# Moving y and its states ahead of the next chunk's scores, with the states in a bank of the w_out parts

## The chip, the cores and the metric

The kernel runs on one core of one Trainium2 chip. The metric is the device time in microseconds of one execution. Engines are named as in the profile: PE is TensorE, DVE is VectorE, ACT is ScalarE, POOL is GpSimd, SP is SyncE.

## The reference

A gated linear recurrence is followed by a two-layer block. Cut to what matters:

```python
batch, n_heads, seq, head_dim = (4, 8, 768, 48)
for t in range(S):
    state = alpha[:, :, t, :, None] * state + np.einsum('bhd,bhe->bhde', k[:, :, t], v[:, :, t])
    y[:, :, t] = np.einsum('bhd,bhde->bhe', q[:, :, t], state)
x = np.ascontiguousarray(y.transpose(0, 2, 1, 3)).reshape(B * S, H * D)   # 3072 x 384
h = x @ w_in                                                              # 384 -> 2048
g = h * (1.0 / (1.0 + np.exp(-h)))
out = g @ w_out                                                           # 2048 -> 384
```

## The kernel before

The recurrence is cut into 24 chunks of 128 tokens (6 along the sequence, times 4 batch entries; chunk n belongs to batch n mod 4). For a chunk the kernel works in stages, each a function:

- `products(n)` and `quotient(n)` build decayed keys and queries on VectorE (transposes at L708, scans at L734 and L764, products at L749, L751 and L770);
- `flip(n)` and `land(n)` turn the keys through a VectorE transpose (L780) and two transfers by way of DRAM, into `kn`;
- `scores(n)` multiplies keys by queries on TensorE, in tiles of 48 rows by 64 columns (the profile shows `ps_a<-p,kp 48*64`). ScalarE copies the result to `g` (L818, L821), GpSimd masks it (L825), and ScalarE scales the state `st` (L836);
- `values(n)` makes y: `g` times v and the old state times the queries, in tiles 128*32 (`ps_a<-g,vn` and `ps_a<-p,st`). ScalarE copies y to `xt` (L863);
- `states(n)` multiplies v by `kn`, also in tiles 128*32 (`ps_a<-vn,kn`), into a PSUM bank, and two VectorE adds (L880) put it onto `st`. The last four chunks need no states.

The two layers work on groups of four chunks. They are cut into pieces of a size: a piece of `enter` (the w_in side; 12 matmuls of 128x256 into banks `ps_m`) and a piece of `leave` (the w_out side; 16 matmuls of 128x192 into the two banks `ps_o`). Both are fast matrix-multiplication schemes with fewer products and more sums; the sums run mostly on VectorE (L958, L1033, L1047, L582 to L587). One `leave` has seven pieces, and two halves of a group have one `leave` each. Its bank use is: parts 1, 3 in bank 0; 2 in bank 1; 4 and 6 in bank 1; 5 and 7 in bank 0.

PSUM has eight banks: three `ps_a` for the recurrence, three `ps_m`, two `ps_o`.

The order is written out by hand. The outer loop runs over steps of four slots. In a slot come first the recurrence's stages of that slot, then `fill(step, slot)`, which issues pieces from a list until a due amount of work is reached. From the ninth chunk on, the slots of a step hold:

```python
stages = [[(land, 1), (scores, 1)], [(products, 0)], [(quotient, 0)],
          [(values, 1), (states, 1), (flip, 0)]]
```

The second number is the lag: at step s, `scores` treats chunk s-1. `marks` gives the slots at which a phase of the list ends; in the later phases 28 pieces, `leave` and `enter` in turn, are spread over 16 slots. A piece also has a chunk count that must have been bridged (its y made) before it may run. VectorE also audits the inputs in the spare time (L697, issued by `audits`). From the ninth chunk on TensorE is held to the order of the program (`keep_in_program_order`); the instructions of the other engines are put in order by a scheduler that works from estimated times, except where they are held as well.

Of the kernel before, what the change touches and what calls it, by code (L numbers as in the profile page):

```python
# [355 lines left out]
def quotients(  # L356
# [38 lines left out]
    C = 128  # L395
# [6 lines left out]
    NT = B * NCH  # L402
    CH = C // 2
    W = C + 1
    GB = 4
# [26 lines left out]
    def out_bank(i, n):  # L432
        return outs[i].tile([128, 512], F32, name="ps_o")[:, 0:n]

    def ps_attn(n=C):
        return ps_a.tile([128, 512], F32, name="ps_a").rearrange("p (j c) -> p j c", c=n)
# [18 lines left out]
    NA = 2 * GB  # L455
# [133 lines left out]
    def sums_w(pair, upto):  # L589

        r = slice(2 * pair, 2 * pair + 2)
        while sums_done[pair] < min(upto, len(SUMS_W)):
            to, sa, a, sb, b = SUMS_W[sums_done[pair]]
            tc.keep_in_program_order(
                combine(block_w(to)[:, r], sa, block_w(a)[:, r], sb, block_w(b)[:, r]))
            sums_done[pair] += 1
# [246 lines left out]
    def values(n):  # L843
# [17 lines left out]
        if e == 0:  # L861
            xts[half] = xtp.tile([128, NKT, TB], F32, name="xt")
        act.copy(xts[half][:, :, e * C : (e + 1) * C], py[:, 0:NKT])  # L863
    def states(n):
        c = ctxs.pop(n)
        ci, b, vn = c["ci"], c["b"], c["v"]
        if ci < NCH - 1:

            ps = ps_attn()
            for j in range(NP):  # L870
                for i in range(4):
                    r = slice(32 * i, 32 * i + 32)
                    kn = c["kn"][:, j, r] if n < NA else c["kn"][:, i, 32 * j : 32 * j + 32]
                    pe.matmul(ps[r, j, 0:D], lhsT=kn, rhs=vn[:, 2 * j + i // 2, 0:D],
                              start=True, stop=True)
            for u in range(2):
                r = slice(64 * u, 64 * u + D)
                s, x = st[b][r, :, u, :], ps[r, :, 0:D]
                if ci > 0:
                    dve.tensor_tensor(s, x, s, ALU.add)  # L880
                else:
                    act.copy(s, x)
# [28 lines left out]
    def enter_plain(grp, h, pair):  # L911

        if h == 0:
            g_tiles(grp, pair)
        xt = xts[2 * grp + h]
        for f in range(8 * pair, 8 * pair + 8, 2):
            ps = bank(f // 2 % 3).rearrange("p (e n) -> p e n", e=2)
            for e in range(2):
                for t in range(NKT):
                    pe.matmul(ps[:, e, :], lhsT=w_in[:, t, (f + e) * 128 : (f + e + 1) * 128],  # L920
                              rhs=xt[:, t, :], start=(t == 0), stop=(t == NKT - 1))
            q, i = divmod(f, 4)
            act.activation(gts[grp, h, pair][:, i : i + 2, q % 2, :], ps, AF.Silu)  # L923
            if grp == 1 and pair == h == 0:
                differences(f // 2)
                differences(4 + f // 2)
            if grp > 0 and f % 8 == 6:
                side_by_side(grp, h, pair)
            yield
# [94 lines left out]
    def cells(grp, h, pair, m, k):  # L1024

        return gts[grp, h, pair][:, k::2, :, m * C : (m + 1) * C]
# [8 lines left out]
    def leave(grp, h):  # L1035


        def product(ps, m, k, w, first=False):
            for i in range(HF):
                q = i // 2  # L1040
                x = gts[grp, h, q // 2][:, 2 * (i % 2) + k, q % 2, m * C : (m + 1) * C]
                pe.matmul(ps, lhsT=x, rhs=w[:, i], start=(first and i == 0), stop=(i == HF - 1),
                          skip_group_check=True)

        def subtract(to, x, y):
            for pair in range(NQ // 2):
                dve.tensor_tensor(cells(grp, h, pair, *to), cells(grp, h, pair, *x),  # L1047
                                  cells(grp, h, pair, *y), ALU.subtract)

        def store(m, c, x, y=None):  # L1050
            ci, b = divmod(GB * grp + 2 * h + m, B)
            o = opool.tile([128, HO], F32, name="o")
            if y is None:
                act.copy(o, x)
            else:
                dve.tensor_tensor(o, x, y, ALU.add)  # L1056
            r = b * S + ci * C

            (gps if grp < NG - 1 else nc.sync).dma_start(out[r : r + C, c * HO : (c + 1) * HO], o)  # L1059

        u1, u2, u3, u4 = [rpool.tile([128, HO], F32, name=f"u{j}") for j in range(4)]
        steps = iter(range(7))

        def done():
            if 2 * grp + h in (1, 2):
                sums_w(2 * grp + h - 1, 4 * next(steps) + 4)

        def new(i):
            return out_bank(i, HO)

        a, b = new(0), new(1)
        product(a, 0, 0, b11, True)
        act.copy(u1, a)
        subtract((0, 0), (1, 0), (0, 0))
        done()
        yield
        product(b, 1, 0, t1, True)
        act.copy(u4, b)  # L1078
        done()
        yield  # L1080
        product(a, 0, 1, b21)
        store(0, 0, a)
        subtract((0, 1), (0, 1), (0, 0))
        done()
        yield
        b = new(1)
        product(b, 0, 0, t2, True)
        dve.tensor_tensor(u2, b, u1, ALU.add)
        subtract((1, 0), (1, 1), (0, 0))
        dve.tensor_tensor(u2, u2, u4, ALU.add)  # L1090
        done()
        yield
        a = new(0)
        product(a, 0, 1, b22, True)
        store(0, 1, a, u2)
        done()
        yield
        product(b, 1, 0, b12)
        dve.tensor_tensor(u3, b, u1, ALU.add)
        store(1, 1, u3, u4)  # L1100
        done()
        yield
        a = new(0)
        product(a, 1, 1, t4, True)
        store(1, 0, a, u3)
        done()
        yield
# [13 lines left out]
    def plain(grp, h, pair):  # L1121
        return (enter_plain(grp, h, pair), 12, 2 * (2 * grp + h) + 2)

    def group(grp):
        return [[(enter(grp, pair), 12, GB * grp + GB)] * 7 for pair in range(2)]

    def output(grp):
        return [[(leave(grp, h), 12, GB * grp + GB)] * 7 for h in range(2)]

    def both(x, y):  # L1130
        for i in range(max(len(x), len(y))):
            pieces.extend(x[i : i + 1] + y[i : i + 1])

    pieces = []
    for h in range(2):
        for pair in range(2):
            pieces += [plain(0, h, pair)] * 4
    pieces += [plain(1, 0, 0)] * 4 + [(leave(0, 0), 12, GB)] * 7
    phases = [len(pieces)]
    pieces += [plain(1, 1, 0)] * 4  # L1140
    both([(leave(0, 1), 12, GB)] * 7, [plain(1, 0, 1)] * 4 + [plain(1, 1, 1)] * 4)
    phases.append(len(pieces))
    before = output(1)
    for grp in range(2, NG):
        sums = sums_x(grp)
# [11 lines left out]

    def go_on():

        nonlocal done  # L1160
        next(pieces[done][0], None)
        done += 1

    audits = audit()
    done, bridged = 0, 0
    STEPS = NT + 1
    SLOTS = 4

    marks = [2 * SLOTS + 2] + [(GB * i + 2 * GB) * SLOTS + 3 for i in range(len(phases))]

    def settle():

# [29 lines left out]

    for step in range(STEPS):
        if step == 1:
            load(NIN)
        stages = [[(scores, 1)], [(products, 0)], [(values, 1)], [(states, 1)]]
        if step == 1:

            stages = stages[1::-1] + stages[2:]
        elif step >= NA:  # L1210
            stages = [[(land, 1), (scores, 1)], [(products, 0)], [(quotient, 0)],
                      [(values, 1), (states, 1), (flip, 0)]]
        for slot, group in enumerate(stages):
            for stage, lag in group:
                n = step - lag
                if not 0 <= n < NT:
                    continue
                stage(n)
                if stage is values:
                    bridged = n + 1  # L1220
                if stage is states and n + 1 + NIN < NA:
                    load(n + 1 + NIN)
                if stage is states and n + NV < NT:
                    load_v(n + NV)
            if step * SLOTS + slot == (NA + 1) * SLOTS - 1:
                x = decayed.rearrange("p (o i c) -> p o i c", o=2, c=C)
                for r, o in later:
                    gps.memset(x[r, o, :, 0:CH], 0.0)
            fill(step, slot)
            if step * SLOTS + slot >= NA * SLOTS - 1 and conv_done[1] == NFT and not late:  # L1230
                settle()
    while next(audits, 0) is None:
        go_on()
# [13 lines left out]
    for _ in range(5):  # L1247
        go_on()
    ps = ps_attn()[0:1, 0, 0:1]
# [64 lines left out]
```

## Time and profile before

| | us |
|---|---|
| median of 3 runs | 556.86 |
| lowest, highest | 556.4, 557.57 |
| profiled execution, its own time | 557.26 |
| span of that execution in the profile | 555.5 |

The page gives the busy time of each engine as a share of the span. A line of the timeline gives start and duration in microseconds, engine, line of the kernel, operation, output and inputs, for a matmul the tile (rows*columns of the array in use), shapes, and how many instructions were merged into the line; in brackets the idle time ahead of it and what ended it. A matmul's end is modelled, so the distance between two starts says more than a duration. A line of the waits gives who waited for whom, the sum in microseconds, how often, and the longest.

### The profile page before, as it was taken

The page shows a single profiled execution, that of the slowest core. Times are in us where ns is not written, and L with a number is a line of the kernel's source. Part 1 is how long each engine was busy: PE and PEld are TensorE (multiplying, and loading weights), DVE is VectorE, ACT ScalarE, POOL GpSimd, SP SyncE. Part 2 cuts the span into 40 slices and gives each one's busy share as a digit, 9 for nine tenths or more (in the row PEclk, how much of TensorE's full clock was granted, in tenths as well). Part 3 has the DMA queues.
Part 4 walks back from the last instruction along what each step waited for, and adds up shares of the span by engine and source line. Part 5 has one row for each costly group of instructions (what it writes and reads, how often), then busy time and mean ns, then how long its engine had stood idle before and what let it go on. Part 6 is the DMA issues. An engine that isn't in the chain of part 4 may idle for free. (4 is left out here: it accounts for less than half of the span.)

```text
span 555.5 us, 12640 instructions
## 1 busy us (share of the span) xinstructions
PE 541.4 (97%) x5026; PEld 489.7 (88%) x5026; DVE 445.4 (80%) x801; ACT 208.5 (38%) x466; POOL 76.1 (14%) x146
## 2 busy tenths in 40 slices
PE   6999999999999999999999999999999999999996
PEld 4788887998899999899999999988998999999996
DVE  5897788974999899997998986998884796945431
ACT  2556653223333253353353353344263342332100
POOL 3210000222210212021011021021121000001000
PEclk9999999999999999999999999999999999999999
DMA  9998971164454625355545654617642135500000
GB/s 215 246 249 210 232 195 33 47 161 116 117 136 125 159 63 138 86 145 149 139 112 139 193 139 120 191 27 183 170 137 91 54 91 169 172 11 22 10 24 30
DMA packets 99217, 70.09 MB, mean 126 GB/s; under 512 B 56272, under 2 KB 88656, under 8 KB 99152
## 3 DMA queue, kind: packets, MB, share of 16 engines
q1 hardware_dynamic: 97232, 65.30, 45.1%
q0 software_dynamic: 1920, 3.93, 2.0%
q8 instruction: 40, 0.66, 0.5%
q14 instruction: 25, 0.20, 0.1%
HBM read 61.34 MB, written 7.86 MB: 125 GB/s over the span
## 5 line engine op out<-in xcount | busy, mean ns | idle before, releaser
L388 PE MATMUL ps_o<-w_out,g 128*128 128x192 f32 x768 | 134.0, 328 | 0.5 <-DVE o L1056 0.5
L388 PEld LDWEIGHTS ps_o<-w_out,g 128*128 128x128 f32 x768 | 125.6, 190 | 3.5 <-DVE o L1056 1.0
L388 PE MATMUL ps_m<-xt,w_in 128*128 128x256 f32 x480 | 113.6, 383 | 1.5 <-ACT xt L863 1.1
L388 PEld LDWEIGHTS ps_m<-xt,w_in 128*128 128x128 f32 x480 | 89.1, 190 | 14.4 <-ACT xt L863 1.6
L388 PE MATMUL ps_o<-wt,g 128*128 128x192 f32 x576 | 99.7, 326 | 0.0
L388 PEld LDWEIGHTS ps_o<-wt,g 128*128 128x128 f32 x576 | 95.1, 190 | 1.6 <-issue 0.2
L388 PE MATMUL ps_m<-xc,w_in 128*128 128x256 f32 x288 | 70.7, 382 | 0.0
L388 PEld LDWEIGHTS ps_m<-xc,w_in 128*128 128x128 f32 x288 | 53.7, 190 | 7.0 <-DVE g L958 0.3
L1047 DVE TENSOR_TENSOR g<-g 128x512 f32<-128x512 f32 x72 | 50.1, 709 | 8.3 <-PE ps_o L388 8.3
L955 ACT ACTIVATE g<-g 128x1024 f32<-128x1024 f32 x32 | 33.1, 1056 | 61.2 <-DVE g L958 61.1
L1059 POOL DMA_DIRECT2D out_dram<-o x40 | 22.0, 551 | 219.5 <-DVE o L1056 113.7
L825 POOL TENSOR_SCALAR_AFFINE_SELECT g<-g 64x256 f32<-64x256 f32 x64 | 34.9, 546 | 124.4 <-ACT g L818 105.7
L388 PE MATMUL ps_m<-xc,wx 128*128 128x256 f32 x192 | 50.1, 383 | 1.0 <-DVE xc L586 1.0
L950 ACT COPY g<-ps_m 128x512 f32<-128x512 f32 x64 | 36.6, 588 | 37.0 <-PE ps_m L388 36.9
L388 PEld LDWEIGHTS ps_m<-xc,wx 128*128 128x128 f32 x192 | 35.2, 190 | 5.2 <-ACT u L1078 1.2
L958 DVE TENSOR_TENSOR g<-ps_m,g 128x512 f32<-128x512 f32 x56 | 37.1, 683 | 3.2 <-PE ps_m L388 2.7
L734 DVE TENSOR_TENSOR_SCAN u<-al,one 128x516 f32<-128x516 f32 x24 | 29.8, 1240 | 11.9 <-ACT al L731 11.6
L923 ACT ACTIVATE g<-ps_m 128x512 f32<-128x512 f32 x32 | 19.1, 597 | 41.7 <-PE ps_m L388 41.4
L950 ACT COPY part<-ps_m 128x512 f32<-128x512 f32 x32 | 18.9, 590 | 38.0 <-PE ps_m L388 24.0
L697 DVE TENSOR_REDUCE seen<-bits 128x1 f32<-128x512 int32 (+1 forms) x33 | 26.3, 823 | 5.7 <-DMA bits<-in_moe_w_in_dram 5.7
L764 DVE TENSOR_TENSOR_SCAN p<-al,inv 128x516 f32<-128x516 f32 x24 | 29.9, 1247 | 1.0 <-PE ps_a L388 0.3
L1056 DVE TENSOR_TENSOR o<-ps_o,u 128x192 f32<-128x192 f32 x24 | 8.5, 355 | 25.7 <-PE ps_o L388 22.8
(129 smaller groups left out, 648.5 us busy)
## 6 DMA issues: line engine op xcount, KB each, us to landing
bits<-in_moe_w_in_dram SPq DMA_DIRECT2D x24, 512.0 KB, 4.7
bits<-in_moe_w_out_dram SPq DMA_DIRECT2D x16, 384.0 KB, 3.9
at<-in_alpha_dram SPq DMA_DIRECT2D x64, 96.0 KB, 2.5
kt<-in_k_dram SPq DMA_DIRECT2D x64, 96.0 KB, 2.6
qt<-in_q_dram SPq DMA_DIRECT2D x64, 96.0 KB, 2.7
bits<-in_alpha_dram SPq DMA_DIRECT2D x9, 512.0 KB, 4.0
out_dram<-o POOLq DMA_DIRECT2D x40, 96.0 KB, 2.4
flips<-turn SPq DMA_DIRECT2D x12, 256.0 KB, 2.4
```

The lines of the kernel that those rows point to most:

```text
L388: in_order(nc.tensor.matmul(*args, **kw))
L697: dve.tensor_reduce(seen[kind][which][:, i : i + 1], x, axis=AX, op=op, apply_absolute_value=True))
L734: dve.tensor_tensor_scan(u[:, end - 1 :: -1], sg[:, end:0:-1], one[:, end:0:-1], 0.0, ALU.mult, ALU.add)
L764: dve.tensor_tensor_scan(p[:, 0:end], sg[:, 0:end], iv[:, 0:end], 0.0, ALU.mult, ALU.add)
L825: gps.affine_select(x, x, pattern=[[0, NP], [1, CH]], compare_op=ALU.is_ge, fill=0.0, base=0, channel_multiplier=-1)
L923: act.activation(gts[grp, h, pair][:, i : i + 2, q % 2, :], ps, AF.Silu)
L950: act.copy(to, ps)
L955: act.activation(x, x, AF.Silu)
L958: dve.tensor_tensor(to, a, b, op)
L1047: dve.tensor_tensor(cells(grp, h, pair, *to), cells(grp, h, pair, *x), cells(grp, h, pair, *y), ALU.subtract)
L1056: dve.tensor_tensor(o, x, y, ALU.add)
L1059: (gps if grp < NG - 1 else nc.sync).dma_start(out[r : r + C, c * HO : (c + 1) * HO], o)
```

## The change

From step 10 on, `values(n)` and `states(n)` have lag 2 and stand at the head of slot 0, immediately ahead of `land` and `scores` of the next chunk; before they stood in slot 3 of the step before, with one call of `fill` between. `states` then takes its bank from the w_out parts' two banks instead of from `ps_a`: bank 0 where three, four or five parts of the current `leave` have been issued, else bank 1. A counter `left` keeps how many that are. Where one or four parts have been issued and the next piece is again a part of w_out, that piece is issued first. There is one more step, and the marks from the second on move by one slot.

```diff
-    def states(n):
+    def states(n, behind=False):
...
-            ps = ps_attn()
+            if behind:
+                ps = out_bank(0 if left in (3, 4, 5) else 1, 512).rearrange("p (j c) -> p j c", c=C)
+            else:
+                ps = ps_attn()
...
+    leaves = []
+
+    def last(grp, h):
+        leaves.append(leave(grp, h))
+        return [(leaves[-1], 12, GB * grp + GB)] * 7
...
-        nonlocal done
+        nonlocal done, left
+        if pieces[done][0] in leaves:
+            left = left % 7 + 1
         next(pieces[done][0], None)
         done += 1
...
-    STEPS = NT + 1
+    STEPS = NT + 2
...
-    marks = [2 * SLOTS + 2] + [(GB * i + 2 * GB) * SLOTS + 3 for i in range(len(phases))]
+    marks = [2 * SLOTS + 2] + [(GB * i + 2 * GB) * SLOTS + 3 + (i > 0) for i in range(len(phases))]
...
         elif step >= NA:
-            stages = [[(land, 1), (scores, 1)], [(products, 0)], [(quotient, 0)],
-                      [(values, 1), (states, 1), (flip, 0)]]
+            lag = 2 if step > NA else 1
+            y = [(values, lag), (states, lag)]
+            stages = [[(land, 1), (scores, 1)], [(products, 0)], [(quotient, 0)], [(flip, 0)]]
+            stages[0 if lag == 2 else 3][0:0] = y
...
-                if not 0 <= n < NT:
+                if not 0 <= n < NT or lag == 2 and n < NA:
                     continue
-                stage(n)
+                if stage is values and lag == 2 and left in (1, 4) and pieces[done][0] in leaves:
+                    go_on()
+                if stage is states:
+                    states(n, lag == 2)
+                else:
+                    stage(n)
```

More of the change, by code (lines that the diff above doesn't have):

```diff
@@ L1125, in group @@
         return [[(enter(grp, pair), 12, GB * grp + GB)] * 7 for pair in range(2)]
+    leaves = []
+    def last(grp, h):
+        leaves.append(leave(grp, h))
+        return [(leaves[-1], 12, GB * grp + GB)] * 7
     def output(grp):
-        return [[(leave(grp, h), 12, GB * grp + GB)] * 7 for h in range(2)]
+        return [last(grp, h) for h in range(2)]
     def both(x, y):
@@ L1137, in quotients @@
             pieces += [plain(0, h, pair)] * 4
-    pieces += [plain(1, 0, 0)] * 4 + [(leave(0, 0), 12, GB)] * 7
+    pieces += [plain(1, 0, 0)] * 4 + last(0, 0)
     phases = [len(pieces)]
     pieces += [plain(1, 1, 0)] * 4
-    both([(leave(0, 1), 12, GB)] * 7, [plain(1, 0, 1)] * 4 + [plain(1, 1, 1)] * 4)
+    both(last(0, 1), [plain(1, 0, 1)] * 4 + [plain(1, 1, 1)] * 4)
     phases.append(len(pieces))
@@ L1164, in quotients @@
     audits = audit()
-    done, bridged = 0, 0
-    STEPS = NT + 1
+    done, bridged, left = 0, 0, 0
+    STEPS = NT + 2
     SLOTS = 4
-    marks = [2 * SLOTS + 2] + [(GB * i + 2 * GB) * SLOTS + 3 for i in range(len(phases))]
+    marks = [2 * SLOTS + 2] + [(GB * i + 2 * GB) * SLOTS + 3 + (i > 0) for i in range(len(phases))]
     def settle():
```

## The prediction

> **What bounds the kernel now.** I read the page first (busy shares), then the timeline of TensorE over one step, then its waits, then the timeline of VectorE behind the same step.
>
> ```profile
> PE 541.4 (97%) x5026; PEld 489.7 (88%) x5026; DVE 445.4 (80%) x801; ACT 208.5 (38%) x466; POOL 76.1 (14%) x146
> ```
>
> TensorE is full almost throughout, but its busy time is modelled, so I look at the distances between starts. One step in the middle:
>
> ```profile
> 327.90 2.76 PE L388 MATMUL ps_o<-w_out,g 128*128 128x192 f32 x16
> 330.50 1.89 PE L388 MATMUL ps_m<-xc,w_in 128*128 128x256 f32 x8
> 332.23 1.03 PE L388 MATMUL ps_m<-xt,w_in 128*128 128x256 f32 x4
> 333.09 2.76 PE L388 MATMUL ps_o<-wt,g 128*128 128x192 f32 x16
> 335.79 1.08 PE L388 MATMUL ps_a<-g,vn 128*32 128x128 f32 x32
> 336.68 0.84 PE L388 MATMUL ps_a<-p,st 128*32 128x128 f32 x24
> 337.34 0.52 PE L388 MATMUL ps_a<-vn,kn 128*32 128x48 f32 x32
> 337.80 1.13 PE L388 MATMUL ps_m<-xc,wx 128*128 128x256 f32 x4
> 338.76 1.89 PE L388 MATMUL ps_m<-xc,w_in 128*128 128x256 f32 x8
> 340.58 0.90 PE L388 MATMUL ps_a<-p,kp 48*64 48x128 f32 x32
> ```
>
> The first column is the start. Inside full-array work the pitch is steady: 8 matmuls of 256 columns in 330.50 to 332.23, 1.73 us or 0.216 each; 16 of 192 in 327.90 to 330.50, 2.60 us or 0.1625 each. The three groups 128*32 are y and states of chunk 18; the group 48*64 is the scores of chunk 19. Between them stands one piece of 12 matmuls, from 337.80 to 340.58: 2.78 us where 12 x 0.216 is 2.60. So 0.19 us is lost at its two borders, about half on entering (the first matmul's weights are not loaded ahead) and half on leaving. The same stretch in the steps where it is a piece of w_out (316.39 to 319.19) takes 2.80 for 2.60, 0.20 lost. TensorE waits for others very little after 140 us:
>
> ```profile
> PE ps_m L388 <- DVE xc L586: 1.0, 1, 1.0
> PE ps_a L388 <- DVE p L770: 0.5, 1, 0.5
> PE ps_m L388 <- DVE g L958: 0.4, 1, 0.4
> ```
>
> Measured as starts against pitch these are 1.2 us at 367, 0.55 at 143 and 0.93 around 229. So the bound is TensorE's own stream; what shortens it shortens the run, and what makes it wait lengthens the run.
>
> VectorE is the engine next to it, and runs behind:
>
> ```profile
> 336.56 1.16 DVE L708 STREAM_TRANSPOSE al<-at 128x512 f32<-128x512 f32 x1
> 337.75 1.23 DVE L734 TENSOR_TENSOR_SCAN u<-al,one 128x516 f32<-128x516 f32 x1
> ...
> 339.51 1.23 DVE L764 TENSOR_TENSOR_SCAN p<-al,inv 128x516 f32<-128x516 f32 x1
> 340.66 0.70 DVE L880 TENSOR_TENSOR st<-ps_a,st 48x192 f32<-48x192 f32 x2
> ```
>
> The two adds of L880 read the states' bank. TensorE finished it by 337.80; they end at 341.36, 3.56 us later. Today nothing waits for them soon.
>
> **What the Trainium skill says.** "TensorEngine Tiling (Array Packing)", Key Properties: changing the tiling mode drains TensorE. The trace agrees: 0.19 to 0.20 us at the borders of each full-array stretch. "TensorE: Matmul & The Clock Gate", Part 2: a weight load can be pulled ahead of running matmuls, matmuls keep their order. The trace agrees: no load cost shows inside a stretch, only at its start. "PSUM — Partial Sum Buffer", PSUM bank collisions: guard by bank and quadrant, not by address. So a w_out product must wait until VectorE has read the states out of its bank; no line of before shows that wait. "Perfetto Trace Analysis", Identifying the Most-Contended Engine: matmul busy share is a poor measure; hence the starts.
>
> **The change part by part.**
>
> *Removed.* Per chunk TensorE today leaves full-array work twice: for y+states and for scores. With y(n), states(n), scores(n+1) back to back, it leaves once. The full stretch between goes and its matmuls join a neighbour at pitch. The merged pairs are y(8) with scores(9) to y(22) with scores(23): 15. Gain 15 x 0.193 = 2.9 us. The drain from 128*32 to 48*64 stays: both groups keep their present lengths (2.01 and 0.83 us). No trace row has these two modes touching, so I bound it: a free switch would also save the tile side's drain, about 0.11 us (the first w_out start comes 0.15 after the last four states matmuls begin, these groups of four being 0.04 apart), 1.6 us in all; a switch dearer by 0.1 would cost 1.5 us. I take zero.
>
> *Moved.* y and states come one slot later; SP's transfers behind states (the three of v, for two chunks ahead) and the ScalarE copy of xt go with them. v is needed two steps later as before; the four kn transfers of `land` now stand right behind states, with a whole step before their reader. The POOL masks have 7 pieces, not 6, between scores and y. `quotient`, `products` and `flip` now come 2 pieces earlier in a step (one piece, not three, between scores and products), so scores(n+1) is later relative to its inputs. All lie beside TensorE's 20.5 us per step. The marks move by a slot with y, so each step still has 7 pieces. Cost nil; if VectorE were late this is where it would first show. An extra step at the end makes the last phase's first fills 4 instead of 1, from pieces that the loop after would issue anyway: nil.
>
> *Added: a wait.* States sit in a w_out bank, and the next product into it waits for L880; everything of TensorE queues behind that product, in order, and after it ScalarE and VectorE. Pieces alternate w_out, w_in. At 28 pieces per 16 slots, odd steps end with seven w_out parts done: bank 1 is free, and its next user is two w_out parts away: 0.83 (scores) + 2.60 + 0.11 + 2.60 = 6.1 us after states. The lags of L880 there are 4.0, 4.6, 2.3, 3.4 and 3.3 us (chunks 11 to 19): no wait. Even steps end with four done: bank 0 is free, but the fifth part wants it after scores and one w_in piece: 0.83 + 2.71 = 3.54 us. The lags of before, from the end of states to the end of L880, are 5.00 (chunk 12), 1.65 (14), 4.19 (16), 3.56 (18). Waits: 1.46 + 0 + 0.65 + 0.02 = 2.1 us. Chunk 8 has the same spacing, but there TensorE itself waits for p at 143 and L880 follows 0.8 us behind; nil. Chunks 20 to 23 have no states. Against that, a wait at chunk 12 lets VectorE catch up by 1.46 just ahead of the 0.93 us that TensorE lost to it around 229: that goes, minus 0.9. Net +1.2 us. Bounds: 0 if L880 lands earlier in VectorE's order, 5 if one more scan (1.23) gets ahead of it each time.
>
> *Sum* against the profiled execution's own 557.26 (span 555.5 and 1.8 around it): 557.26 - 2.9 + 1.2 = 555.6. That execution was 0.4 above the median of 556.86, so 555.2 against the median.
>
> **The rivals.**
>
> R1, *the bank gives all back*: the waits come to 2 to 4 us net; 556 to 558. For it: VectorE has 79.3 us of work in the 84 us from 190 to 274. Against: the waits of before, carried over, come to 2.1.
>
> R2, *slower, by the same bank*: in even steps one more 1.23 us scan is ordered ahead of L880. Lags 6.2, 2.9, 5.4, 4.8; waits 2.7 + 0 + 1.9 + 1.3 = 5.9, minus 0.9: 557.26 - 2.9 + 5.0 - 0.4 = 559.0. It decides at a mean lag of about 4.5 us in even steps; before has 3.6. For it: the transposes and scans of later chunks already run ahead of L880, and products now stand two pieces nearer. Against: at chunks 16 and 18 the whole chain al, u, p is already ahead.
>
> R3, *no waits at all* (VectorE's earlier quotient and flip leave it nearer to TensorE): 553.6 to 554.
>
> R4, *it does not do what it says*: if TensorE's order were the scheduler's, the groups need not touch. In this part of the kernel TensorE is kept in program order, so I give it no weight of its own.
>
> **How the numbers follow.** Forecast (554.2 to 555.7) 0.45, R3 0.11, R1 0.24, R2 and slower 0.20. A measurement can tell about 0.2%, 1.1 us. Faster by more: 0.56; within: 0.24; slower: 0.20. Range from 553.3 (R3) to 558.9 (R2's size).
>
> **What would show it.** Right: 128*32 groups followed at once by 48*64, 15 times; full stretches of 28 pieces' pitch with one 0.19 border per step; waits of TensorE's ps_o for `st` L880 of about a microsecond in even steps only. Wrong: such waits over 1.5 us each, or in odd steps; a longer 48*64 group (the switch costs); new waits for xc or g at L958 over those of before.

## The result, and the profile after

The change makes the kernel slower: 571.7 us median (571.32 to 572.26, 5 runs) against 556.4 us before (555.96 to 557.57, the three runs of the table above and two more); the ratio is 1.027, 95% interval 1.0259 to 1.0281. The profiled execution took 572.26 us with a span of 570.5, against 557.26 and 555.5 before: 15.0 us more of span.

From the page after, the busy shares, and the group of matmuls whose idle time has grown (busy time, mean ns of one, then the idle time before it and what ended most of it):

```profile
PE 543.5 (95%) x5026; PEld 493.3 (86%) x5026; DVE 445.3 (78%) x801; ACT 209.6 (37%) x466; POOL 74.2 (13%) x146
...
L388 PE MATMUL ps_m<-xc,wx 128*128 128x256 f32 x192 | 52.4, 397 | 10.2 <-DVE xc L586 10.2
```

The work is what it was; TensorE waited for the sums of x (`xc`), 10.2 us where it was 1.0. TensorE's own waits (total, times, longest) say the same and name the next one:

```profile
PE ps_m L388 <- DVE xc L586: 10.2, 2, 5.8
...
PE ps_a L388 <- DVE p L770: 2.9, 2, 1.9
```

TensorE's timeline from y of chunk 15 on, where group 3 starts:

```profile
274.26 1.08 PE L388 MATMUL ps_a<-g,vn 128*32 128x128 f32 x32
275.15 0.84 PE L388 MATMUL ps_a<-p,st 128*32 128x128 f32 x24
275.81 0.52 PE L388 MATMUL ps_o<-vn,kn 128*32 128x48 f32 x32
276.26 0.90 PE L388 MATMUL ps_a<-p,kp 48*64 48x128 f32 x32
277.10 2.87 PE L388 MATMUL ps_o<-w_out,g 128*128 128x192 f32 x16
279.80 1.89 PE L388 MATMUL ps_m<-xc,w_in 128*128 128x256 f32 x8
281.53 1.03 PE L388 MATMUL ps_m<-xc,wx 128*128 128x256 f32 x4
282.39 2.76 PE L388 MATMUL ps_o<-wt,g 128*128 128x192 f32 x16
290.93 1.62 PE L388 MATMUL ps_m<-xc,wx 128*128 128x256 f32 x3 [5.78 <-DVE xc L586]
```

Its first four lines are the change: y, states (now in `ps_o`) and scores stand together, and take 2.84 us in all, as long as they took apart. The last line is the loss: by the pitch of the 16 matmuls ahead of it that matmul was due at 284.99, and it started at 290.93.

The balance from the starts of TensorE's matmuls, each against the pitch of its kind (0.2165 us for 256 columns, 0.1625 for 192), before and after, in us:

| | before | after | difference |
|---|---|---|---|
| full-array stretches after 126 us (each costs 0.19 at its borders) | 33 | 18 | -2.9 |
| starts of groups 3 and 4: what the stretch with the wait for `xc` takes over the 18.37 of such a stretch undisturbed (before: over 15.77, in one of the two) | 1.2 | 8.2 + 6.3 | +13.3 |
| scores waiting for p (chunks 9, 10, 11) | 0.55 | 1.9 + 0.2 + 1.1 | +2.7 |
| smaller waits | | | +0.7 |
| last matmul's start | 550.45 | 564.22 | +13.8 |
| from there to the end of the span | 5.07 | 6.31 | +1.2 |

VectorE's timeline after, at the same place:

```profile
278.49 0.36 DVE L883 TENSOR_TENSOR st<-ps_o,st 48x192 f32<-48x192 f32 x1
...
283.89 0.69 DVE L1050 TENSOR_TENSOR g<-g 128x512 f32<-128x512 f32 x1
284.50 1.21 DVE L697 TENSOR_REDUCE seen<-bits 128x1 f32<-128x1024 f32 x1
285.63 0.42 DVE L582 TENSOR_TENSOR xc<-xt 128x256 f32<-128x256 f32 x1
...
290.38 0.41 DVE L586 TENSOR_TENSOR xc<-xc,xt 128x256 f32<-128x256 f32 x1
```

and before, where y of chunk 15 stood 1.8 us earlier:

```profile
276.76 0.42 DVE L582 TENSOR_TENSOR xc<-xt 128x256 f32<-128x256 f32 x1
...
281.80 0.42 DVE L586 TENSOR_TENSOR xc<-xc,xt 128x256 f32<-128x256 f32 x1
...
284.27 1.21 DVE L697 TENSOR_REDUCE seen<-bits 128x1 f32<-128x1024 f32 x1
```

L586 at 290.38 and 281.80 is the sixth sum, which TensorE's wait ends on. Before, the reduce of an audit followed the sums; after, the sums start as soon as the reduce is over. At chunk 19 it is the same: two reduces at 375.41 to 376.6, first sum at 376.60. VectorE is not idle meanwhile, and it does not wait for the reduce's transfer there: that was issued at 271.59, and such transfers land in 4.0 us in the median; the reduce simply stands that late in VectorE's order.

Where that comes from in the code: `fill` calls the audit at even slots, ahead of its pieces, and it lists the nine sums of x once y of the group's last chunk has been listed. Before, that y stood in slot 3, an odd one; now it stands in slot 0, an even one, so the reduce is listed directly ahead of the nine sums, which are held in program order.

Behind these two waits TensorE also ran slow. The starts of 256-column matmuls were 0.427 us apart, not 0.2165, for 4.6 us after the first wait and 3.4 us after the second. Of the 14.5 us of the two stretches the waits themselves are 5.9 and 4.6, and what came behind them 2.3 and 1.7. The windows show it in the granted clock (the third figure from the end, 1.00 and 0.88):

```profile
190.00:274.00 84.00, 83.48 (x864) 77.03 (x861) 77.58 (x142) 34.43 (x81) 11.99 (x23) 1.00 0.46 122
274.00:303.00 29.00, 23.22 (x219) 20.98 (x218) 24.96 (x44) 11.04 (x25) 4.42 (x6) 0.88 0.47 122
```

### The profile page after: what moved, and what is told of

It reads as the page before. It is cut to its first block, busy times and chain, and to the rows that moved or that the text cites. A ratio compares the mean times of both kernels' runs of the same rounds, so it can differ in the third digit from the quotient of the medians.

```text
span 570.5 us, 12640 instructions
## 1 busy us (share of the span) xinstructions
PE 543.5 (95%) x5026; PEld 493.3 (86%) x5026; DVE 445.3 (78%) x801; ACT 209.6 (37%) x466; POOL 74.2 (13%) x146
## 5 line engine op out<-in xcount | busy, mean ns | idle before, releaser
L388 PE MATMUL ps_m<-xc,wx 128*128 128x256 f32 x192 | 52.4, 397 | 10.2 <-DVE xc L586 10.2
L388 PEld LDWEIGHTS ps_m<-xc,w_in 128*128 128x128 f32 x288 | 55.1, 194 | 7.0 <-DVE g L961 0.3
L1050 DVE TENSOR_TENSOR g<-g 128x512 f32<-128x512 f32 x72 | 48.6, 688 | 12.4 <-PE ps_o L388 12.4
L388 PEld LDWEIGHTS ps_m<-xc,wx 128*128 128x128 f32 x192 | 36.7, 198 | 15.1 <-issue 10.7
L825 POOL TENSOR_SCALAR_AFFINE_SELECT g<-g 64x256 f32<-64x256 f32 x64 | 33.0, 515 | 103.2 <-ACT g L818 88.5
L388 PE MATMUL ps_a<-g,vn 128*32 128x128 f32 x768 | 28.0, 282 | 0.4 <-POOL g L813 0.3
```

Of the source, the lines that this page charges most:

```text
L388: in_order(nc.tensor.matmul(*args, **kw))
L825: gps.affine_select(x, x, pattern=[[0, NP], [1, CH]], compare_op=ALU.is_ge, fill=0.0, base=0, channel_multiplier=-1)
```

## The experiments

Theories: A, the sums stand behind an audit's reduce. B, VectorE is late since `products` and `quotient` come two pieces earlier in a step. C, the states' bank holds TensorE up. D is on the smaller loss: the scores of chunks 9 to 11 wait for p because a w_out part now runs ahead of y, and its subtractions come ahead of p on VectorE.

**Audit behind the pieces** (on the changed kernel)

```diff
-        if at % 2 == 0 and step > 3 * GB + 2:
-            next(audits, None)
         while work_at[done + 1] <= due and pieces[done][2] <= bridged:
             ...
+        if at % 2 == 0 and step > 3 * GB + 2:
+            next(audits, None)
```

> The changed kernel with one edit: in fill, the audit is issued after the pieces of the slot, not ahead of them. Theory A (at the start of a phase the nine sums of x stand behind an audit's reduce in VectorE's held order, and the reduce behind much else): the two long waits of TensorE for xc (5.9 and 4.6 us, and some 4 us at half the pitch behind them) go, 13 us less, 557 to 559 us, about as before. Theory B (VectorE is late because products and quotient come two pieces earlier in a step): the waits for xc stay above 3 us each, 568 us or more. Theory C (the states' bank holds TensorE up): no change, 571.

Measured: 558.07 us (556.62 to 560.05, 12 runs), 1.0022 times the kernel before (1.0011 to 1.0032). 13.6 us of the loss are gone with this edit alone; TensorE's order and GpSimd's are the same as in the changed kernel. Its VectorE at the place in question:

```profile
277.24 0.36 DVE L883 TENSOR_TENSOR st<-ps_o,st 48x192 f32<-48x192 f32 x1
277.63 0.43 DVE L582 TENSOR_TENSOR xc<-xt 128x256 f32<-128x256 f32 x1
```

The sums follow the state's add at once. No wait for `xc` is left, and no slow pitch. A holds; B and C do not explain the loss.

**Audit's reduces not held** (on the changed kernel: `keep_in_program_order` taken off the reduces of `audit`)

> The changed kernel with one edit: the audit's reduces are no longer held in program order, so the scheduler may put the sums ahead of them. Theory A: the long waits for xc go, 556 to 560 us; a new order of VectorE elsewhere can cost or gain a few us. Theory B: waits for xc stay, 568 us or more. Theory C: 571.

Measured: 574.58 us (574.24 to 576.91, 4 runs), 1.0313 (1.0298 to 1.0328). That is against what A was taken to say. The sums still come right behind the reduce:

```profile
283.11 1.21 DVE L696 TENSOR_REDUCE seen<-bits 128x1 f32<-128x1024 f32 x1
284.23 0.41 DVE L582 TENSOR_TENSOR xc<-xt 128x256 f32<-128x256 f32 x1
```

So the reduce's own hold isn't the tie. That left two forms of A: the hold on the sums, or the place in the list alone.

**Sums of x not held** (on the changed kernel: `keep_in_program_order` taken off the sums in `sums_x`, audits left ahead)

> The changed kernel with the sums of x not held in program order, the audits left as they are, ahead of the pieces. Theory A, first form (the hold on the sums ties them to the instruction listed ahead of them, the reduce; that is why freeing the reduces alone did nothing): the sums start within 5 us of y at the two phase starts, no long wait for xc, 556 to 561 us. Second form (the scheduler takes VectorE's work by its place in the list, hold or no hold): the sums still follow the reduce, 568 us or more.

Measured: 558.85 us, 1.003 (1.0019 to 1.004). The first sum starts 6.2 and 4.6 us after y at the two starts, not 11.4 and 11.0, and the long waits are gone. The tie is the hold on the sums: it keeps them behind the reduce that is listed ahead of them.

**The kernel before with audits at odd slots** (`at % 2 == 1`)

> The kernel before with one edit: audits at odd slots, so that one falls on slot 3, in which a phase starts there; y, states and products stay in their old places. Theory A: the loss appears without the change: waits of TensorE for xc of 4 to 6 us at two phase starts (about 274 and 358 us), 565 to 571 us. Theory B: nothing was moved but audits, 556 to 557.5. Theory C: 556 to 557.5.

Measured: 560.19 us, 1.0061 (1.0045 to 1.0076). A part of the loss appears without the change, smaller than expected: waits for `xc` of 0.5 and 2.9 us. The sums again start right after the reduce, 7.0 and 10.5 us after y, where they took 5.3 us at chunk 19 before; the first group's reduce happened to stand earlier, right behind the states' adds, and no slow pitch followed the wait of 2.9 us.

**The kernel before with the marks alone moved** (`+ 3 + (i > 0)`)

> The kernel before with one part of the change: the marks from the second on are a slot later, so that the later phases start in slot 0, an even one with an audit ahead of its pieces; y and states stay in slot 3. Theory A: the long waits for xc are here too, 567 to 572 us (no gain from the borders). Theory B: products are two pieces nearer here too, so a loss as well, spread over all steps and not on the two phase starts alone. Theory C: 556 to 557.5, since states stay in the old banks.

Measured: 560.08 us, 1.0059 (1.0043 to 1.0075). The edit did not do what it was meant to. The nine sums hold no matmuls, so `fill` lists them as soon as the pieces of the phase before are used up and y of the group's last chunk has been listed. Here that is still in slot 3, where y stayed, and so a slot ahead of the audit. VectorE shows the reduce behind the last sum:

```profile
285.49 0.41 DVE L586 TENSOR_TENSOR xc<-xc 128x256 f32<-128x256 f32 x1
285.82 1.21 DVE L697 TENSOR_REDUCE seen<-bits 128x1 f32<-128x1024 f32 x1
```

So the number expected from A did not apply. The run shows that the later marks alone do not put the sums behind an audit; it takes y in slot 0. The one wait for `xc` is 1.1 us, as before the change. The 3 us have other places (1.4 us for `kn`, 0.7 for a bank of `ps_o`, and more).

**Audits at odd slots** (on the changed kernel)

> The changed kernel with the audits at odd slots: the one ahead of a phase's start now stands a slot earlier, ahead of y. Theory A (the sums stand behind an audit's reduce that is itself far behind its transfer): a reduce one slot nearer to its place leaves the sums some 2.6 us of TensorE's time earlier than in the changed kernel, so the waits for xc shrink to 0 to 3 us each and the half pitch behind them goes: 557 to 563 us. Theory B (products nearer): no change, 571.

Measured: 558.22 us, 1.0025 (1.0016 to 1.0034). The waits for `xc` shrink to 0.6 and 0.9 us. A slot's distance is enough, as A has it.

**States in a `ps_a` bank** (audit behind the pieces; `ps = ps_attn()` in all cases)

> The changed kernel with the audit behind the pieces, and the states in one of the three ps_a banks, as before the change, not in a w_out bank. y, the states and the two banks of scores want four of three: the second scores bank is the one that ScalarE has to copy y out of, which it does 0.5 to 1 us after y ends, while states take 0.45. Expected: a wait of TensorE for the copy of xt of 0.3 to 1 us at each of 12 chunks, 4 to 10 us in all, 562 to 568. If the copy is in time: 558.

Measured: 569.63 us (567.11 to 573.01, 5 runs; the profile is of the slowest), 1.022 (1.0204 to 1.0235), 11.6 more than with the audit behind alone and above the 562 to 568 expected.

```profile
PE ps_a L388 <- ACT xt L863: 6.7, 4, 2.4
```

The wait comes at 4 chunks rather than 12, but with 0.9 to 2.6 us each, and with slow pitch behind two of them. So with the states in a `ps_a` bank the merge costs more than it removes.

**y moved from chunk 12 on only** (audit behind the pieces; `NA + 4` for `NA` in the two conditions on the lag, `(i > 1)` in the marks)

> The changed kernel with the audit behind the pieces, and y moved ahead of the scores only from chunk 12 on: 11 merges, not 15. Theory D (the waits of 1.9, 0.2 and 1.1 us for p at the scores of chunks 9 to 11 come from the w_out part that now runs ahead of y, whose subtractions enter VectorE ahead of p): these waits go back to the 0.55 us of before, 2.7 us won, 4 borders of 0.19 lost: 1.9 us less than with the audit behind alone, 555.5 to 556.5. If they have another cause: 558 to 559.5.

Measured: 559.67 us, 1.0049 (1.0037 to 1.0062). The total missed both expectations. The waits for p did go back to 0.6 us at chunk 9 and none at 10 and 11, but the later pieces fell on other slots, and the states of chunk 12 waited 2.1 us for their bank, which VectorE (L1059) had not yet read out. Slow pitch followed that wait. So the run does not decide on D.

**All marks a slot later** (audit behind the pieces)

```diff
-    marks = [2 * SLOTS + 2] + [(GB * i + 2 * GB) * SLOTS + 3 + (i > 0) for i in range(len(phases))]
+    marks = [2 * SLOTS + 2] + [(GB * i + 2 * GB) * SLOTS + 4 for i in range(len(phases))]
```

> The changed kernel with the audit behind the pieces, and every mark a slot later, the first one too, so that at chunk 8 the piece ahead of y is again one of w_in, as before the change, and the first w_out part follows the scores of chunk 9. Theory D (that part's subtractions stand ahead of p on VectorE): the wait of 1.9 us at the scores of chunk 9 falls to 0.5 us or less; those of 0.2 and 1.1 at chunks 10 and 11 may stay. 1.4 to 2.7 us less than with the audit behind alone: 555.4 to 556.7, at or below the kernel before. If the wait comes from merging as such (y and states of chunk 8 no longer give VectorE time, since scores follow at once): 1.5 us or more of it stays, 558.

Measured: 555.97 us (555.36 to 557.19, 15 runs) against 557.01 before, 0.9981 (0.9973 to 0.9989): 1.0 us, 0.2%, below the kernel before. In the changed kernel the scores of chunk 9 wait for p:

```profile
142.71 0.52 PE L388 MATMUL ps_o<-vn,kn 128*32 128x48 f32 x32
145.09 0.90 PE L388 MATMUL ps_a<-p,kp 48*64 48x128 f32 x32 [1.85 <-DVE p L770]
```

On VectorE two subtractions of the w_out part stand ahead of it there:

```profile
139.96 0.69 DVE L1050 TENSOR_TENSOR g<-g 128x512 f32<-128x512 f32 x1
...
142.42 0.68 DVE L1050 TENSOR_TENSOR g<-g 128x512 f32<-128x512 f32 x1
143.02 1.08 DVE L708 STREAM_TRANSPOSE turn<-qt 128x512 f32<-128x512 f32 x1
...
144.28 0.66 DVE L770 TENSOR_TENSOR p<-turn,p 128x512 f32<-128x512 f32 x1
```

Before the change none did, and p started 1.3 us earlier:

```profile
141.85 1.11 DVE L708 STREAM_TRANSPOSE turn<-qt 128x512 f32<-128x512 f32 x1
142.99 0.69 DVE L770 TENSOR_TENSOR p<-turn,p 128x512 f32<-128x512 f32 x1
```

With all marks a slot later the scores follow at once, and the first w_out part stands behind them:

```profile
139.08 0.52 PE L388 MATMUL ps_o<-vn,kn 128*32 128x48 f32 x32
139.61 0.90 PE L388 MATMUL ps_a<-p,kp 48*64 48x128 f32 x32
140.44 2.87 PE L388 MATMUL ps_o<-w_out,g 128*128 128x192 f32 x16
```

The wait at chunk 9 is down to less than 0.1 us. Others of 1.1 and 1.3 us stand at chunks 11 and 12, so the waits for p are 2.5 us in all, where the kernel with the audit behind the pieces has 3.3. The spans of the two profiled executions differ by 0.9 us; of the 2.1 us between the medians the rest is not accounted for. The kernel before with all its marks a slot later was not run, so how much of the gain is due to the merge is not shown either.

**The same marks with audits at odd slots**

> The same step of the marks on the changed kernel with the audits at odd slots. Theory D: the wait at chunk 9 goes here too, 555.5 to 557. Else 558.

Measured: 557.31 us, 1.0009 (1.0 to 1.0017), a little above the 555.5 to 557 expected. The wait at chunk 9 is gone here too; waits for `xc` of 0.6 and 0.9 us stay.

## Why the prediction was wrong

It said 555.2 us, 553.3 to 558.9; measured were 571.7.

*Removed: right.* 15 merges, 15 stretches fewer, 0.19 each: 2.9 us. The two modes touching cost nothing of their own: y, states and scores take 2.01 and 0.83 us as before, and the stretches between have one pair of borders left. TensorE kept the order of the program, so R4 is out.

*Moved: this step failed.* "The marks move by a slot with y, so each step still has 7 pieces. Cost nil". The count of pieces was right, but a slot is not only a place for pieces: even slots issue an audit first, and the nine sums of x come behind y wherever it stands. The step priced the transfers, the masks and the products, and left out what `fill` lists on VectorE between y and the pieces. Moving y from slot 3 to slot 0 put a late reduce directly ahead of held sums: the waits for `xc` at the two phase starts came to 10.5 us and what followed them at half pitch to 4.0, where before there was one wait of 1.2. The prediction named new waits for `xc` as a sign against it, and had seen L586 wait 1.0 us before; it gave that wait no mechanism by which it could grow.

The same step let one more thing pass as free. With y of chunk 8 behind the pieces of slot 3, a w_out part came ahead of it, where before it followed. At chunk 9 the part's subtractions (L1050) stood ahead of p on VectorE. The scores of chunks 9 to 11 waited 3.2 us in all, not 0.55. Moving the part behind the scores removed the wait at chunk 9; those at 11 and 12 stay unexplained.

*Added, the wait for the bank: mechanism right, size wrong.* The lags of the states' adds in even steps, from the end of states, were 3.65, 2.09, 1.65 and 1.65 us after, for 5.00, 1.65, 4.19 and 3.56 before, against the 3.54 allowed. So one wait remained, 0.27 us at chunk 12, for the 2.1 forecast. The 0.93 us of VectorE's lateness around 229 us did not go away either; there the changed kernel loses about as much. R1 and R2, which rest on that bank, are both out, and R3 was nearest on the bank. Slower was among the chances, but it came by another mechanism than the one given for it.

*The end.* This term was put at nil too. In all runs with y moved the span ends 6.1 to 6.3 us after the last matmul's start, in the three without it 5.1 to 5.3. SyncE's next instruction after its branch (L1300) comes 2.65 us later in the kernel with all marks a slot later; before, 0.5 us. The two instruction queues moved 65 packets in the three kernels without the move and 66 or 67 in all others. Whether one has to do with the other was not tested.

*Slips without effect.* TensorE's step is 20.5 and 21.4 us in turn, not 20.5. Before the change the listing has two pieces, not three, between scores and products. R3 is given as 553.6 to 554, so the 553.3 of the range is not its figure.

*Left open.* Why VectorE's order puts the reduce so late. The 12.9 us from the issue of its transfer are no delay of this place: a call of the audit lists the reduce of the transfer that the call two slots before it issued, and from slot 2 to slot 0 the next steps show 13.3 and 12.6 us. But at the two starts the reduce stands 5.7 and 5.0 us behind the end of the states' adds, behind subtractions and work of the next chunk that are listed after it. In the kernel before with audits at odd slots it follows them at once at the first start, and by 3.9 us at the second. No run changed that by itself.

## What to carry to other kernels

Before moving a boundary in a schedule written out by hand, list everything that the new slot issues beside the moved work, on every engine, and everything that may only be listed once the moved work is. Look for what is held in order there: here the hold bound the sums to a neighbour in the list that they did not need. Price a merge by the border it removes, and then the neighbours it gives to the work around it; here 2.9 us of borders brought some 16 us of waits and half pitch, and with two small edits of places the kernel came out 1.0 us below the one before. A wait of TensorE of some microseconds should be priced with the slow pitch that may follow it.

## What the hardware showed that was not expected

After waits of 5.9 and 4.6 us TensorE ran at half its pitch (0.427 for 0.2165 us) for 4.6 and 3.4 us. "TensorE: Matmul & The Clock Gate", Part 1, of the Trainium skill describes a clock gate that halves the clock after an idle window of about 3.4 us, a window that runs freely. The half pitch agrees. The length of the waits does not: half pitch also followed waits of 1.9 us (at the scores of chunk 9 in the kernel with states in `ps_a`, 0.427 us apart for some six matmuls), 2.1 us (y moved from chunk 12 on) and 3.0 us (the audit's reduces not held), all shorter than that window. And the same wait of 1.9 us in the changed kernel had none behind it, nor had 2.85 us in the kernel before with audits at odd slots. A window that does not start with the wait could tell equal waits apart, but not explain why such short ones are enough; neither was tested by itself.
